# Attention stage on whole 1152-column PSUM regions, with unsplit float32 projections

## The chip, the cores and the metric

The kernel runs on one core of one Trainium2 chip. The metric is the device time of one execution in microseconds (us). The core has a matrix engine (TensorE, "PE" in the profile; "PEld" are its weight loads), a vector engine (VectorE, "DVE"), a scalar engine (ScalarE, "ACT"), GpSimd ("POOL") and a queue engine that issues DMAs (SyncE, "SP"). SBUF is the on-chip memory of 128 partitions; PSUM is the small memory that TensorE writes into, of 8 banks, each 512 float32 wide. TensorE's clock has two levels, 1.2 and 2.4 GHz; the profile gives the granted clock of a stretch as a share of the higher one.

## The reference

Batch 8, 8 heads, 576 tokens, head dimension 64. The stage that changes is the first, a linear attention:

```python
def phi(x):                                   # x: (b, h, 576, 64), w_phi: (64, 128)
    proj = einsum('bhsd,df->bhsf', x, w_phi)
    proj = proj - max(abs(proj), axis=-1, keepdims=True)
    return concatenate([exp(proj), exp(-proj)], axis=-1)
q_p, k_p = phi(q), phi(k)
kv  = einsum('bhsf,bhsd->bhfd', k_p, v)
z   = sum(k_p, axis=2)
num = einsum('bhsf,bhfd->bhsd', q_p, kv)
den = einsum('bhsf,bhf->bhs', q_p, z)[..., None] + 1e-6
out = num / den
```

Two feed-forward stages follow (a gated one with a 576 x 576 spatial product, then a low-rank token mixing and a channel network of width 2048). All is float32.

## The kernel before, in words

The heads are worked two at a time: 32 pairs, one turn of the loop in `attention` (L516) for each. A framework turns the program into five in-order instruction streams: it plans an order by program order, readiness and its own costs, allocates tiles from named rings (a tag with `bufs` buffers) and places the waits. `issue_after(x)` keeps what stands under it behind instruction x.

A pair's 576 tokens are 4 full tiles of 128 tokens and a tail of 64; the tails of both heads share one 128-token tile, so a pair has 9 blocks of 128 tokens x 128 features, 1152 columns in all. In one turn for pair p the program issues, in this order: the loads of q and k of pair p+1; `queries(p)`; `key_values(p-1)`; `keys(p)`; `outputs(p-1)`; `transposed_queries(p)`; `finish(p-2)` on GpSimd; `reciprocals(p-1)`; and one weight job (a piece of a later stage's weights: DMA, unpacking at L55 to L72, split), of which there are 29.

- `split_pair` (L364) makes a high and a low float32r part of each 128 x 640 input, one copy on VectorE and one subtraction on GpSimd.
- `project` (L373) multiplies with a block-diagonal weight for both heads at once (256 columns), three matmuls for each full tile (high-high, low-high, high-low) and three of 128 columns for the tail: 15 matmuls for q (tile names pq) and 15 for k (pk). They go to PSUM in three parts of 512, 512 and 128 columns; each part has one absolute maximum (L392) and one subtraction (L397) on VectorE.
- `keys` (L404): two exponentials for each part on ScalarE into kp. `key_values` (L445): 18 float32 matmuls into pkv, then a split into kv.
- `transposed_queries` (L415): 9 transposes by TensorE (pt), then for each of three parts and both signs an exponential in float32r (L440), the same in float32 (L441) and their difference on VectorE (L442), into qp.
- `outputs` (L468): 24 float32r matmuls (pn) in four groups of six, each copied out by ScalarE (L482). The denominators take a round through DRAM (L484, L494, L496); `finish` multiplies (L507) and stores x by one DMA (L513).

PSUM is one pool for the whole kernel, with two rings of four one-bank buffers: "a" (pq, pk, pt and the float32 exponentials e) and "b" (pkv, pn).

Of the kernel before, what the change touches and what calls it, by code (L numbers as in the profile page):

```python
# [9 lines left out]
F32 = mybir.dt.float32  # L10
F32R = mybir.dt.float32r
# [7 lines left out]
P = 128  # L19
# [59 lines left out]
class Mixer:  # L79
# [3 lines left out]
    def __init__(self, tc, ctx, aps):  # L83
        self.tc, self.nc, self.ctx = tc, tc.nc, ctx
        self.__dict__.update(aps)
        self.B, self.NP = self.qT.shape[:2]
        self.D, self.F = self.w_phi.shape[0] // 2, self.w_phi.shape[1] // 3
        self.S = self.U.shape[0]
# [244 lines left out]
    def alloc_attention(self, es):  # L333
        tc, nc = self.tc, self.nc
        D, F = self.D, self.F
        self.af = es.enter_context(tc.tile_pool(name="af", bufs=1))
        ap = self.ap = es.enter_context(tc.tile_pool(name="ap", bufs=1))

        self.wph, self.wst = (
            [ap.tile([P, n], F32R, name=f"{m}{i}") for i in range(2)]  # L340
            for m, n in (("wph", 2 * F), ("wst", F))
        )
        wz = self.stage("wz", 3 * F)
        nc.scalar.dma_start(wz, self.w_phi)
        self.split(self.wph[0], self.wph[1], wz[:, : 2 * F], ehi="dve", elo="dve")
        self.split(self.wst[0], self.wst[1], wz[:, 2 * F :])
        self.st = {}
# [15 lines left out]

    def split_pair(self, p, w):  # L364
        x = [
            self.ap.tile([P, self.NST * P], F32R, tag=f"{w}s{i}", name=f"{w}s{i}_{p}", bufs=1)
            for i in range(2)
        ]
        lo = self.split(x[0], x[1], self.st[p][w], ehi="dve", elo="pool" if p else "dve")
        self.last[3] = lo.ins  # L370
        self.st[p][w] = x

    def project(self, p, w):  # L373


        nc, F, NF = self.nc, self.F, self.NF
        hi, lo = self.st[p][w]
        res = []
        for t0 in range(0, self.NST, 2):
            tiles = range(t0, min(t0 + 2, self.NST))  # L380
            n = sum(2 if t < NF else 1 for t in tiles)
            pa = self.psum(f"p{w}{p}_{t0}").rearrange("p (u f) -> p u f", f=F)
            for t in tiles:
                cols = slice(t * P, (t + 1) * P)
                at = 2 * (t - t0)
                out, ws = (
                    (pa[:, at : at + 2, :], self.wph) if t < NF else (pa[:, at, :], self.wst)
                )
                for i, (x, y) in enumerate(((hi, 0), (lo, 0), (hi, 1))):
                    nc.tensor.matmul(out, x[:, cols], ws[y], start=(i == 0), stop=(i == 2))  # L390
            m = self.ap.tile([P, 4, 1], F32, tag="m", name=f"m{w}{p}_{t0}", bufs=6)
            nc.vector.tensor_reduce(  # L392
                out=m[:, :n, :], in_=pa[:, :n, :], op=ALU.max, axis=AX.X,
                apply_absolute_value=True,
            )
            s = self.ap.tile([P, 4, F], F32, tag=f"s{w}", name=f"s{w}{p}_{t0}", bufs=3)
            nc.vector.tensor_tensor(  # L397
                out=s[:, :n, :], in0=pa[:, :n, :],
                in1=m[:, :n, :].to_broadcast([P, n, F]), op=ALU.subtract,
            )  # L400
            res.append((2 * t0, n, s))
        return res

    def keys(self, p):  # L404
        nc, F = self.nc, self.F
        kp = self.ap.tile([P, 2 * self.NF + 1, 2, F], F32, tag="kp", name=f"kp{p}", bufs=1)
        for u0, n, s in self.project(p, "k"):
            for i, sign in enumerate((1.0, -1.0)):
                nc.scalar.activation(kp[:, u0 : u0 + n, i, :], s[:, :n, :], AF.Exp, scale=sign)  # L409
        self.st[p]["kp"] = kp  # L410
# [4 lines left out]
    def transposed_queries(self, p):  # L415
        nc, F, NF, S, tail = self.nc, self.F, self.NF, self.S, self.tail
        pts = [self.psum(f"pt{p}_{j}") for j in range(3)]
        for u0, n, s in reversed(self.st[p]["sq"]):
            for u in range(n):
                t, j = divmod(u0 + u, 2)  # L420
                out = pts[j][:, t * P : (t + 1) * P] if t < NF else pts[2][:, :P]
                nc.tensor.transpose(out, s[:, u, :], self.ident)
        qp = [
            self.ap.tile([P, 2, 2, S], F32R, tag=f"qp{i}", name=f"qp{i}_{p}", bufs=1)
            for i in range(2)
        ]


        for j in (2, 0, 1):
            if j < 2:  # L430
                src = pts[j]
                hi, lo = ([q[:, j, i, : NF * P] for i in range(2)] for q in qp)
                es = [self.psum(f"e{p}_{j}"), src]
            else:
                r3 = lambda a: a.rearrange("p (h s) -> p h s", h=2)
                src = r3(pts[2][:, :P])
                hi, lo = ([q[:, :, i, NF * P :] for i in range(2)] for q in qp)
                es = [r3(pts[2][:, P : 2 * P]), src]
            for i, sign in enumerate((1.0, -1.0)):
                nc.scalar.activation(hi[i], src, AF.Exp, scale=sign)  # L440
                self.last[0] = nc.scalar.activation(es[i], src, AF.Exp, scale=sign).ins  # L441
                nc.vector.tensor_tensor(out=lo[i], in0=es[i], in1=hi[i], op=ALU.subtract)  # L442
        self.st[p]["qp"] = qp

    def key_values(self, p):  # L445
        nc, D, NF = self.nc, self.D, self.NF
        kp, vb = self.st[p]["kp"], self.st[p]["v"]
        D1 = D + 1
        pkv = self.psum(f"pkv{p}", "b")[:, : 4 * D1].rearrange("p (i j d) -> p i j d", i=2, j=2)
        for i in range(2):  # L450
            nc.tensor.matmul(
                pkv[:, i], kp[:, 2 * NF, i, :], vb[:, 2 * NF * D1 :], start=True, stop=False
            )
            for j in range(2):
                for t in range(NF):
                    u = 2 * t + j
                    nc.tensor.matmul(  # L457
                        pkv[:, i, j, :], kp[:, u, i, :], vb[:, u * D1 : (u + 1) * D1],
                        start=False, stop=(j == 1 and t == NF - 1),
                    )  # L460
        kv = [
            self.ap.tile([P, 2, 2, D1], F32R, tag=f"kv{i}", name=f"kv{i}_{p}", bufs=2)
            for i in range(2)
        ]
        self.split(kv[0], kv[1], pkv, elo="dve")
        self.st[p]["kv"] = kv

    def outputs(self, p):  # L468
# [4 lines left out]
        for j in range(2):  # L473
            for c in range(2):
                pn = self.psum(f"pn{p}_{j}_{c}", "b")
                for n, (k, q, i) in enumerate(terms):
                    nc.tensor.matmul(  # L477
                        pn[: D + 1, :HS], kv[k][:, i, j, :],
                        qp[q][:, j, i, c * HS : (c + 1) * HS],
                        start=(n == 0), stop=(n == len(terms) - 1),  # L480
                    )
                nc.scalar.copy(nd[:, j, c, :], pn[: D + 1, :HS])  # L482
# [18 lines left out]
    def finish(self, p, eng):  # L501
# [4 lines left out]
        for j in range(2):  # L506
# [5 lines left out]
            )  # L512
        nc.sync.dma_start(self.xd[b][:, hp, :], x)  # L513
        del self.st[p]

    def attention(self, jobs):  # L516
        n = self.B * self.NP
        late, rest, work = self.NP + 3, [], None
        self.load_pair(0)
        self.split_pair(0, "q")  # L520
        self.split_pair(0, "k")
        for p in range(n + 1):
            if p + 1 < n:
                self.load_pair(p + 1)
            if p < n:
                self.queries(p)
                if p + 1 < n:
                    self.split_pair(p + 1, "q")
            if p:
                self.key_values(p - 1)  # L530
            if p < n:
                self.load_values(p)
                self.keys(p)
                if p + 1 < n:
                    self.split_pair(p + 1, "k")
            if p:
# [482 lines left out]
```

## Time and profile before

| | us |
|---|---|
| median of 3 runs (1825.13 to 1828.86) | 1827.36 |
| the profiled execution | 1825.05 |
| its span, first to last instruction | 1822.9 |
| mean granted clock over the span | 0.976 |

The span is what the trace covers; the 2.15 us beside it lie around it. Times inside the trace count from the span's start. A matmul's duration holds its way through the array and overlaps that of the next, so a stream's cost is read from start to start. A float32 matmul leaves two records and two weight loads, a float32r matmul or a transpose one.

### The profile page before, as it was taken

To read this page: it belongs to the slowest core of one execution; us is meant where nothing else is said; L and a number is where in the kernel's file an instruction comes from. 1 tells how busy PE (TensorE), PEld (TensorE's weight loads), DVE (VectorE), ACT (ScalarE), POOL (GpSimd) and SP (SyncE) were. 2 spreads that over 40 slices of the span, in tenths; PEclk is the share of its full clock that TensorE was granted. 3 is DMA by queue.
4 is the path that set the end of the run, shared out by engine and by line. 5 is a ranking of instruction groups with operands and counts; after the bars stand their busy time and mean duration, and the time that the engine had idled before them with its cause. 6 is when DMAs were issued, how large, how long until landed. Compare 5 with 4: busy or idle time off the path is not lost.

```text
span 1822.9 us, 27191 instructions
## 1 busy us (share of the span) xinstructions
PE 1731.4 (95%) x10632; PEld 1644.4 (90%) x10632; DVE 894.0 (49%) x1750; ACT 648.3 (36%) x1509; POOL 433.4 (24%) x367
## 2 busy tenths in 40 slices
PE   7888888888899999999999999999999999999999
PEld 7787888787898888888889899999999999999999
DVE  6889988788866566665653721211211210211211
ACT  4666665666654443443343411111201201211210
POOL 1445444444434342333332010000000000000000
PEclk8999899999999999999999999999999999999999
DMA  3444444434212332332221620110110110110100
GB/s 121 127 117 129 128 117 135 119 111 122 81 43 76 117 117 94 111 112 90 78 89 56 187 64 1 35 36 1 35 35 1 35 35 1 35 35 4 32 18 18
DMA packets 78468, 132.14 MB, mean 72 GB/s; under 512 B 17090, under 2 KB 39778, under 8 KB 78340
## 3 DMA queue, kind: packets, MB, share of 16 engines
q1 hardware_dynamic: 78196, 130.21, 23.4%
q8 instruction: 84, 1.38, 0.3%
q14 instruction: 44, 0.36, 0.1%
q10 hardware_dynamic: 144, 0.20, 0.0%
HBM read 93.38 MB, written 36.85 MB: 71 GB/s over the span
## 4 chain that ended last, share of the span: by engine, by line
PE 60%; DMA 7%; DVE 6%; ACT 3%; POOL 2%; issue 1%; SPq 0%; DVEq 0%; POOLq 0%; ACTq 0%
PE pc L582 22%; PE ph L582 21%; DMA raw_c<-in_w_ch 5%; PE pv L582 4%; PE px L582 3%; PE pu L582 3%; PE pt L785 1%; PE pz L582 1%; PE py L789 1%; PE pkv L457 1%; DMA den<-nd 1%; PE pn L477 1%; ACT kp L409 1%; POOL xs L617 1%; DVE qp L442 1%
## 5 line engine op out<-in xcount | busy, mean ns | idle before, releaser
L582 PE MATMUL pc<-h,w 128*128 128x384 f32 x2304 | 403.8, 335 | 0.0
L582 PEld LDWEIGHTS pc<-h,w 128*128 128x128 f32 x2304 | 402.0, 188 | 0.0
L582 PE MATMUL ph<-us,w 128*128 128x384 f32 x2244 | 391.0, 334 | 0.0
L582 PEld LDWEIGHTS ph<-us,w 128*128 128x128 f32 x2244 | 389.2, 188 | 0.0
L833 ACT ACTIVATE h<-ph 128x384 fp32r<-128x384 f32 x187 | 91.9, 492 | 631.3 <-PE ph L582 631.3
L834 DVE SCALAR_TENSOR_TENSOR h<-ph,h 128x384 fp32r<-128x384 f32 x187 | 104.2, 557 | 275.2 <-ACT h L833 275.1
L121 POOL TENSOR_TENSOR us<-u,us 128x384 fp32r<-128x384 f32 x48 | 49.3, 1061 | 682.3 <-ACT us L118 673.3
L869 DVE TENSOR_TENSOR u<-pc,u 128x384 f32<-128x384 f32 x48 | 25.5, 557 | 364.1 <-PE pc L582 364.1
L457 PE MATMUL pkv<-v,kp 128*128 128x65 f32 x1024 | 139.6, 296 | 0.0
L457 PEld LDWEIGHTS pkv<-v,kp 128*128 128x128 f32 x1024 | 138.0, 216 | 0.0
L477 PE MATMUL pn<-qp,kv 128*65 128x288 f32 x768 | 119.3, 298 | 7.4 <-DVE kv L121 4.9
L582 PE MATMUL pz<-wt,vn 128*128 128x288 f32 x768 | 112.6, 295 | 1.2 <-DVE u L727 1.2
L477 PEld LDWEIGHTS pn<-qp,kv 128*65 128x65 f32 x768 | 97.9, 137 | 14.4 <-DVE kv L121 10.1
L582 PEld LDWEIGHTS pz<-wt,vn 128*128 128x128 f32 x768 | 105.2, 188 | 2.1 <-DVE u L727 1.9
L440 ACT ACTIVATE qp<-pt 128x128 fp32r<-128x128 f32 (+1 forms) x192 | 93.7, 493 | 35.5 <-DVE qp L442 32.8
L582 PE MATMUL px<-wo,g 128*128 128x512 f32 x384 | 94.1, 403 | 11.7 <-ACT g L118 11.7
L582 PEld LDWEIGHTS pu<-xs,wi 128*128 128x128 f32 x768 | 102.7, 188 | 0.7
L582 PE MATMUL pu<-xs,wi 128*128 128x288 f32 x768 | 103.2, 295 | 0.0
L582 PEld LDWEIGHTS px<-wo,g 128*128 128x128 f32 x384 | 72.9, 194 | 30.4 <-ACT g L118 14.3
L507 POOL TENSOR_TENSOR x<-nd,rec 64x576 f32<-64x576 f32 x62 | 91.9, 1482 | 15.2 <-ACT nd L482 10.2
L582 PE MATMUL pv<-wi,xs 128*128 128x512 f32 x384 | 92.3, 393 | 0.0
L390 PE MATMUL pq<-wph,qs 128*128 128x256 f32 x384 | 72.2, 341 | 17.5 <-DVE qp L442 9.3
(152 smaller groups left out, 2333.2 us busy)
## 6 DMA issues: line engine op xcount, KB each, us to landing
raw_c<-in_w_ch SPq DMA_DIRECT2D x32, 512.0 KB, 4.4
v<-in_v SPq DMA_DIRECT2D x32, 325.0 KB, 3.0
q<-in_qT SPq DMA_DIRECT2D x32, 320.0 KB, 2.9
k<-in_kT SPq DMA_DIRECT2D x32, 320.0 KB, 3.0
rec<-rd SPq DMA_DIRECT2D x32, 288.0 KB, 3.7
xd<-x SPq DMA_DIRECT2D x32, 288.0 KB, 2.1
x<-xd SPq DMA_DIRECT2D x32, 288.0 KB, 3.0
outT<-u SPq DMA_DIRECT2D x48, 192.0 KB, 1.9
```

What stands on the lines that cost most here:

```text
L121: return (nc.gpsimd if elo == "pool" else nc.vector).tensor_tensor(out=lo, in0=src, in1=hi, op=ALU.subtract)
L390: nc.tensor.matmul(out, x[:, cols], ws[y], start=(i == 0), stop=(i == 2))
L409: nc.scalar.activation(kp[:, u0 : u0 + n, i, :], s[:, :n, :], AF.Exp, scale=sign)
L440: nc.scalar.activation(hi[i], src, AF.Exp, scale=sign)
L442: nc.vector.tensor_tensor(out=lo[i], in0=es[i], in1=hi[i], op=ALU.subtract)
L457: nc.tensor.matmul(pkv[:, i, j, :], kp[:, u, i, :], vb[:, u * D1 : (u + 1) * D1], start=False, stop=(j == 1 and t == NF - 1),)
L477: nc.tensor.matmul(pn[: D + 1, :HS], kv[k][:, i, j, :], qp[q][:, j, i, c * HS : (c + 1) * HS], start=(n == 0), stop=(n == len(terms) - 1),)
L507: eng.tensor_tensor(out=x[j * D : (j + 1) * D, :], in0=nd[:D, j].rearrange("p c s -> p (c s)"), in1=rec[:, j * S : (j + 1) * S], op=ALU.mult,)
L582: self.nc.tensor.matmul(out, x, y, start=(start and i == 0), stop=(stop and i == len(terms) - 1))
L833: nc.scalar.activation(h[:, 0, :], ph, AF.Relu)
L834: nc.vector.scalar_tensor_tensor(out=h[:, 1, :], in0=ph, scalar=0.0, in1=h[:, 0, :], op0=ALU.max, op1=ALU.subtract,)
L869: nc.vector.tensor_tensor(out=u[:, f, :], in0=pcs[f], in1=u[:, f, :], op=ALU.add)
```

## The change

The weight is no longer block-diagonal but the 64 x 128 weight stacked twice; q and k are used as they are loaded. Each head is multiplied within its own 64 rows (partitions 0 to 63 or 64 to 127) by one float32 matmul of 128 columns; the tail tile uses all 128 rows. The whole projection lies in one PSUM region of three banks, with one maximum, one subtraction and one exponential per sign over 1152 columns. The transposes fill another three-bank region, in an order that puts the tail between the heads. Of the two differences of the queries' exponentials one goes to GpSimd. The attention's PSUM has a pool of its own: one region "pa" (q, then k), one "pt", and a ring of two banks "b"; the later stages' pool is made after the attention. The store of x becomes three DMAs. The weight jobs stand behind the last exponential and VectorE's difference of the turn.

```diff
-        self.ps = ctx.enter_context(tc.tile_pool(name="ps", bufs=1, space=PSUM))   # __init__
+        self.pp = es.enter_context(tc.tile_pool(name="pp", bufs=1, space=PSUM))    # alloc_attention
+        self.wst = ap.tile([P, F], F32, name="wst")
+        nc.scalar.dma_start(self.wst, self.w_phi)
-    def split_pair(self, p, w):
...
+    def wide(self, name, tag):
+        t = self.pp.tile([P, 12, P], F32, tag=tag, name=name, bufs=1)
+        return t[:, : 2 * self.NF + 1, :]
     def project(self, p, w):
-                for i, (x, y) in enumerate(((hi, 0), (lo, 0), (hi, 1))):
-                    nc.tensor.matmul(out, x[:, cols], ws[y], start=(i == 0), stop=(i == 2))
+        n = 2 * NF + 1
+        pa = self.wide(f"p{w}{p}", "pa")
+        x, ws = self.st[p][w], self.wst
+        for t in range(NF):
+            cols = slice(t * P, (t + 1) * P)
+            for j in range(2):
+                d = slice(j * D, (j + 1) * D)
+                nc.tensor.matmul(
+                    pa[:, j * NF + t, :], x[d, cols], ws[d, :], start=True, stop=True
+                )
+        nc.tensor.matmul(pa[:, 2 * NF, :], x[:, NF * P :], ws, start=True, stop=True)
+        m = self.ap.tile([P, n, 1], F32, tag="m", name=f"m{w}{p}", bufs=2)
+        nc.vector.tensor_reduce(
+            out=m, in_=pa, op=ALU.max, axis=AX.X, apply_absolute_value=True
+        )
+        s = self.ap.tile([P, n, F], F32, tag=f"s{w}", name=f"s{w}{p}", bufs=1)
+        nc.vector.tensor_tensor(
+            out=s, in0=pa, in1=m.to_broadcast([P, n, F]), op=ALU.subtract
+        )
+        return s
     def keys(self, p):
+        s = self.project(p, "k")
+        kp = self.ap.tile([P, 2, 2 * self.NF + 1, F], F32, tag="kp", name=f"kp{p}", bufs=1)
+        for i, sign in enumerate((1.0, -1.0)):
+            nc.scalar.activation(kp[:, i], s, AF.Exp, scale=sign)
     def transposed_queries(self, p):
+        pt = self.wide(f"pt{p}", "pt")
+        for u in (*range(NF), 2 * NF, *range(NF, 2 * NF)):
+            at = u if u < NF else NF if u == 2 * NF else u + 1
+            nc.tensor.transpose(pt[:, at, :], s[:, u, :], self.ident)
+        pt = pt.rearrange("p u f -> p (u f)")
...
+        e = self.ap.tile([P, 2 * S], F32, tag="e", name=f"e{p}", bufs=1)
+        nc.scalar.activation(qp[0][:, 0, :], pt, AF.Exp)
+        nc.scalar.activation(e, pt, AF.Exp)
+        lo = nc.gpsimd.tensor_tensor(out=qp[1][:, 0, :], in0=e, in1=qp[0][:, 0, :], op=ALU.subtract)
+        nc.scalar.activation(qp[0][:, 1, :], pt, AF.Exp, scale=-1.0)
+        self.last[0] = nc.scalar.activation(pt, pt, AF.Exp, scale=-1.0).ins
+        d = nc.vector.tensor_tensor(out=qp[1][:, 1, :], in0=pt, in1=qp[0][:, 1, :], op=ALU.subtract)
+        self.last[1], self.last[2] = d.ins, lo.ins
     def key_values(self, p), outputs(self, p):
-        pkv = self.psum(f"pkv{p}", "b") ... pn = self.psum(f"pn{p}_{j}_{c}", "b")
+        pkv = self.pp.tile([P, 512], F32, tag="b", name=f"pkv{p}", bufs=2)
+                pn = self.pp.tile([P, 512], F32, tag="b", name=f"pn{p}_{j}_{c}", bufs=2)
     def finish(self, p, eng):
-        nc.sync.dma_start(self.xd[b][:, hp, :], x)
+        nc.sync.dma_start(self.xd[b][:D, hp, :], x[:D, :])
+        nc.sync.dma_start(self.xd[b][D:, hp, :full], x[D:, S - full :])
+        nc.sync.dma_start(self.xd[b][D:, hp, full:], x[D:, : S - full])
     def attention(self, jobs):
-            with self.tc.issue_after(self.last[3]):
+            with self.tc.issue_after(self.last[0]), self.tc.issue_after(self.last[1]):
                 if work:
                     work = work()
-                with self.tc.issue_after(self.last[0]):
-                    rest = [f() for f in rest]
+                rest = [f() for f in rest]
     def alloc_moe(self, left, right):
+        self.ps = self.ctx.enter_context(
+            tc.tile_pool(name="ps", bufs=1, space=PSUM, reuse_waits="tile")
+        )
-        return np.block([[w, z, w], [z, w, w]])
+        return np.concatenate([w, w], axis=0)
```

## Rows read from the trace of the kernel before

**Rows 1.** Windows: stretch, length; busy us (records) by engine, clock, DMA share, GB/s.

```profile
24.00:504.00 480.00, 417.68 (x3011) 390.06 (x3011) 409.14 (x799) 301.91 (x769) 209.57 (x151) 0.93 0.40 117
...
1200.00:1400.00 200.00, 200.00 (x1152) 200.00 (x1151) 32.99 (x60) 28.54 (x60) 11.80 (x12) 1.00 0.07 24
```

**Rows 2.** Line 451: ns min/median/max of one, first and last start us.

```profile
L451 PE MATMUL pkv<-v,kp x128: 275/329/587, 16.4 to 510.5; 128*128 128x130 f32 x128
```

**Rows 3.** Timeline of TensorE, one turn at the upper clock: start, us.

```profile
300.11 1.59 PE L390 MATMUL pk<-wph,ks 128*128 128x256 f32 x12
301.54 0.30 PE L477 MATMUL pn<-qp,kv 128*65 128x288 f32 x1
301.67 0.45 PE L390 MATMUL pk<-wst,ks 128*128 128x128 f32 x3
301.96 0.30 PE L422 MATMUL pt<-ident,sq 128*128 128x128 f32 x1
302.14 2.59 PE L477 MATMUL pn<-qp,kv 128*65 128x288 f32 x18
304.57 1.03 PE L422 MATMUL pt<-ident,sq 128*128 128x128 f32 x8
306.71 0.49 PE L451 MATMUL pkv<-v,kp 128*128 128x130 f32 x2 [1.11 <-ACT kp L409]
307.04 1.90 PE L457 MATMUL pkv<-v,kp 128*128 128x65 f32 x16
308.77 0.44 PE L451 MATMUL pkv<-v,kp 128*128 128x130 f32 x2
309.05 1.90 PE L457 MATMUL pkv<-v,kp 128*128 128x65 f32 x16
310.75 0.95 PE L390 MATMUL pq<-wph,qs 128*128 128x256 f32 x6
```

**Rows 4.** Waits of TensorE, 24 to 504 us: total us, times, longest.

```profile
PE pkv L451 <- ACT kp L409: 33.4, 30, 1.2
```

**Rows 5.** Windows of 4 us: a stretch whose clock falls.

```profile
488.00:492.00 4.00, 2.89 (x24) 2.65 (x22) 3.96 (x8) 3.53 (x9) 3.84 (x4) 1.00 0.01 2
...
496.00:500.00 4.00, 4.00 (x20) 4.00 (x20) 2.33 (x6) 3.04 (x7) 0.00 (x0) 0.50 0.06 9
```

**Rows 6.** Tile pt, 600 to 900 us: weight loads of 64 rows; idle before them.

```profile
L785 PEld LDWEIGHTS pt<-ident,x x90: 134/139/144, 642.7 to 897.2; 128*128 128x128 f32 x72, 64*128 64x128 f32 x18
...
  issue: 3.0, 18
```

**Rows 7.** Groups of instructions by form, 24 to 504 us, VectorE: busy us, mean ns.

```profile
L392 DVE TENSOR_REDUCE mq<-pq 128x4 f32<-128x512 f32 x62 | 42.3, 682 | 15.1 <-PE pq L390 14.9
L442 DVE TENSOR_TENSOR qp<-e,qp 128x512 fp32r<-128x512 f32 x60 | 41.2, 687 | 7.4 <-ACT e L441 7.4
L59 DVE SCALAR_TENSOR_TENSOR bits_wi<-raw_wi,bits_wi 128x256 int32<-128x256 int32 x15 | 24.4, 1628 | 0.5
L120 DVE CAST ks<-k 128x640 fp32r<-128x640 f32 x30 | 19.6, 654 | 0.0
L55 DVE TENSOR_SCALAR bits_wi<-raw_wi 128x256 int32<-128x256 int32 x15 | 19.6, 1308 | 0.0
L442 DVE TENSOR_TENSOR qp<-pt,qp 128x128 fp32r<-128x128 f32 x60 | 17.3, 288 | 24.0 <-ACT pt L441 23.9
```

**Rows 8.** The same view, ScalarE.

```profile
L440 ACT ACTIVATE qp<-pt 128x512 fp32r<-128x512 f32 x120 | 72.3, 603 | 0.0
L440 ACT ACTIVATE qp<-pt 128x128 fp32r<-128x128 f32 x60 | 16.4, 274 | 32.8 <-DVE qp L442 32.8
```

**Rows 9.** The same view, GpSimd.

```profile
L121 POOL TENSOR_TENSOR ks<-k,ks 128x640 fp32r<-128x640 f32 x30 | 47.6, 1587 | 4.0 <-PE pn L477 1.8
L121 POOL TENSOR_TENSOR wi<-w_wi,wi 128x256 fp32r<-128x256 f32 x16 | 11.8, 736 | 111.5 <-ACT wi L118 111.5
```

**Rows 10.** The line that stores x, 24 to 504 us: issue ns min/median/max.

```profile
L513 SPq DMA_DIRECT2D xd<-x x29: 326/327/327, 50.6 to 491.8; - x29
```

More of the change, by code (lines that the diff above doesn't have):

```diff
@@ L86, in __init__ @@
         self.B, self.NP = self.qT.shape[:2]
-        self.D, self.F = self.w_phi.shape[0] // 2, self.w_phi.shape[1] // 3
+        self.D, self.F = self.w_phi.shape[0] // 2, self.w_phi.shape[1]
         self.S = self.U.shape[0]
@@ L335, in alloc_attention @@
         D, F = self.D, self.F
+        self.pp = es.enter_context(tc.tile_pool(name="pp", bufs=1, space=PSUM))
         self.af = es.enter_context(tc.tile_pool(name="af", bufs=1))
         ap = self.ap = es.enter_context(tc.tile_pool(name="ap", bufs=1))
[L339 to L346, printed above, removed]
+        self.wst = ap.tile([P, F], F32, name="wst")
+        nc.scalar.dma_start(self.wst, self.w_phi)
         self.st = {}
@@ L362, in load_values @@
         self.st[p]["v"] = vb
-    def split_pair(self, p, w):
[L365 to L371, printed above, removed]
-    def project(self, p, w):
[L376 to L387, printed above, removed]
-                )
-                for i, (x, y) in enumerate(((hi, 0), (lo, 0), (hi, 1))):
-                    nc.tensor.matmul(out, x[:, cols], ws[y], start=(i == 0), stop=(i == 2))
[L391 to L402, printed above, removed]
@@ L415, in transposed_queries @@
     def transposed_queries(self, p):
[L416 to L422, printed above, removed]
+        nc, F, NF, S = self.nc, self.F, self.NF, self.S
@@ L423, in transposed_queries @@
+        s = self.st[p]["sq"]
+        pt = self.wide(f"pt{p}", "pt")
[3 more added lines that the diff above has]
+        pt = pt.rearrange("p u f -> p (u f)")
         qp = [
-            self.ap.tile([P, 2, 2, S], F32R, tag=f"qp{i}", name=f"qp{i}_{p}", bufs=1)
+            self.ap.tile([P, 2, 2 * S], F32R, tag=f"qp{i}", name=f"qp{i}_{p}", bufs=1)
@@ L425, in transposed_queries @@
             for i in range(2)
         ]
[L429 to L442, printed above, removed]
+        e = self.ap.tile([P, 2 * S], F32, tag="e", name=f"e{p}", bufs=1)
@@ L448, in key_values @@
         D1 = D + 1
-        pkv = self.psum(f"pkv{p}", "b")[:, : 4 * D1].rearrange("p (i j d) -> p i j d", i=2, j=2)
+        pkv = self.pp.tile([P, 512], F32, tag="b", name=f"pkv{p}", bufs=2)
+        pkv = pkv[:, : 4 * D1].rearrange("p (i j d) -> p i j d", i=2, j=2)
         for i in range(2):
             nc.tensor.matmul(
-                pkv[:, i], kp[:, 2 * NF, i, :], vb[:, 2 * NF * D1 :], start=True, stop=False
+                pkv[:, i], kp[:, i, 2 * NF, :], vb[:, 2 * NF * D1 :], start=True, stop=False
             )
@@ L457, in key_values @@
                     nc.tensor.matmul(
-                        pkv[:, i, j, :], kp[:, u, i, :], vb[:, u * D1 : (u + 1) * D1],
+                        pkv[:, i, j, :], kp[:, i, j * NF + t, :], vb[:, u * D1 : (u + 1) * D1],
                         start=False, stop=(j == 1 and t == NF - 1),
@@ L512, in finish @@
             )
-        nc.sync.dma_start(self.xd[b][:, hp, :], x)
+        full = self.NF * P
+        nc.sync.dma_start(self.xd[b][:D, hp, :], x[:D, :])
+        nc.sync.dma_start(self.xd[b][D:, hp, :full], x[D:, S - full :])
+        nc.sync.dma_start(self.xd[b][D:, hp, full:], x[D:, : S - full])
         del self.st[p]
@@ L983, in rows, with stacked @@
         )
-    def diagonal(w):
-        z = np.zeros_like(w)
-        return np.block([[w, z, w], [z, w, w]])
+    def stacked(w):
+        return np.concatenate([w, w], axis=0)
     arrays = {
@@ L993 @@
         "v": rows(inputs["v"]),
-        "w_phi": diagonal(inputs["w_phi"]),
+        "w_phi": stacked(inputs["w_phi"]),
         "w_in": inputs["moe_w_in"],
```

14 lines of the change are left out of this document (2 added, 12 removed).

## The prediction

> **What bounds the kernel now.** I read the windows first. From 24 to 504 us, the attention, TensorE is 418 of 480 us busy, VectorE 409, ScalarE 302; at 1200 us TensorE is busy throughout at full clock and the others hardly [rows 1]. So the change can act on the attention alone, and behind it TensorE sets the time: what a turn of the loop gains shows in the total, once for each of 31 intervals.
>
> How long is a turn? Line 451 runs four times for each of 32 pairs, from 16.4 to 510.5 us [rows 2]; its two halves lie 2.06 us apart (306.71 and 308.77), and the two records of one matmul 0.14 [rows 3]. (510.5 - 0.14 - 2.06 - 16.4) / 31 = 15.87 us.
>
> What does TensorE need of it? The timeline of one turn at the upper clock, from start to start [rows 3]: pkv 306.71 to 310.75, 4.04 us. A projection: twelve matmuls of 256 columns in 1.43 (0.12 each), three of 128 in 0.29, together 1.72; there are two, 3.44. Eighteen pn in 2.43, so 24 take 3.24. Eight transposes end 1.03 after their start, the last one's own 0.27 to 0.30 within that: 0.11 each, nine in 0.98. Sum 11.7 us. So 4.2 of 15.87 us are not matmul work. 33.4 us in 30 turns, 1.1 each, are waits of pkv for the key exponentials [rows 4]: a chain from VectorE's subtraction through ScalarE. Another 1.1 is the clock, 0.93 on the mean, 7% of the turn [rows 1]. A fall looks like this: TensorE is 2.89 of 4 us busy from 488 us, at 1.00, and by 496 us it runs at 0.50, the 1.2 GHz level [rows 5]. The other 2.0 are shorter waits. VectorE, 409.14 / 30.2 = 13.5 us a turn, is almost as full as the turn is long, so what stands in its queue is late for TensorE.
>
> **The change part by part.**
>
> *Projection.* 15 float32r matmuls become 8 + 1 float32 ones, 18 records of 128 columns. Nearest rows: records of 130 columns, 0.14 each by the second pair (308.77 to 309.05) and 0.165 by the first (306.71 to 307.04), and records of 65 columns, 0.106 (16 in 1.70) [rows 3]. I take 0.12, nearer the two cheap ones because the 0.165 follows a wait: 18 x 0.12 = 2.16. If the two heads' matmuls, in different rows, ran side by side, a record would cost half of 0.106, the lower end. Going to 64 rows and back: weight loads of 64 rows stood 3.0 us idle in 18 cases, 0.17 each, with no releaser [rows 6]; two changes a projection, 0.34. A projection 2.5, plus 0.78 each, 1.56 a turn. Floor of a turn: 11.7 + 1.56 = 13.3 us.
>
> The Trainium skill, "TensorEngine Tiling (Array Packing)", section Tiling Modes, says that changing the tiling mode drains TensorE. That speaks against this change, and the trace agrees: 0.17 us each [rows 6].
>
> *VectorE.* 687 ns at 512 and 288 at 128 columns [rows 7]: 1.04 ns a column and 0.155 fixed, so 1.35 us at 1152. No row shows one instruction over three banks; bounds are this, and one more fixed part at each of two borders, 1.66. I take 1.35. Maxima and subtractions: 8 x 0.68 + 4 x 0.28 = 6.6 becomes 4 x 1.35 = 5.4. Differences of the queries: 4 x 0.687 + 2 x 0.288 = 3.3 becomes one, 1.35. Two copies, 0.65 at most each, go [rows 7]. Together about 4.3 less: 9.2 us a turn.
>
> *ScalarE.* 603 at 512, 274 at 128 [rows 8]: 1.15 us at 1152 (1.48 with a fixed part for each border). Key exponentials, 4 x 0.60 + 2 x 0.27 = 2.9, become 2.3; queries', 5.9, become 4.6. Of 10.0 us a turn about 8 remain; no bound.
>
> *GpSimd.* 1587 at 640 and 736 at 256 columns [rows 9]: the new difference takes 2.7 us, two of 1.59 go. It is on the way to the outputs, beside two more exponentials (2.3) and VectorE's 1.35, so it hides; uncovered it would add 2.7.
>
> *One region for both projections.* The next projection must wait until the subtraction has read the last. Worked from t = 0, the end of the key subtraction of pair p-1: the query projection (2.5) now stands where TensorE waited for the key exponentials, which end at 2.3; pkv 2.5 to 6.55; maximum and subtraction of q 2.6 to 5.3, under pkv; key projection to 9.05; outputs to 12.3; transposes to 13.3. Query exponentials of p-1 2.3 to 6.9, GpSimd's difference by 7.3, VectorE's by 8.35, both before the outputs. Keys' maximum and subtraction 9.2 to 11.9, 1.4 us ahead of the next projection. So the wait of 1.1 is gone, and late next is VectorE. The weight jobs are held until its difference, 8.35, and two of their instructions alone take 1.31 + 1.63 [rows 7]: they end at 11.3, the key subtraction at 14.0. Plus 0.7 in a turn with such a job.
>
> *Ring of two instead of four.* A group of outputs is 6 x 0.135 = 0.81; its copy must end before the next but one, with 0.81 to spare. ScalarE is idle there in the order above, so nothing; with a query exponential of 1.15 ahead, 0.3 to 0.7.
>
> *Clock.* Idle ahead of pkv is what the fall showed, and that goes; I keep 0.5 of 1.1.
>
> *Stores.* Two more issues a turn, 2 x 0.327 = 0.65 of SP's time [rows 10], hidden as long as no load stands late behind them; 21 us in 32 turns if all did. The moved jobs' loads stand behind them in the same queue. Later stages: nothing, TensorE is full there.
>
> Sum: 13.3 + 0.7 + 0.5 = 14.5 us a turn; (15.87 - 14.5) x 31 = 42.5 us less. From the profiled execution, 1825.05: 1782.5. That execution lies 2.3 below the median of the runs shown; I put the forecast at 1783, a little over the sum.
>
> **The rivals.**
>
> *A, side by side.* The 64-row matmuls overlap: 16 x 0.053 + 2 x 0.12 + 0.34 = 1.4 a projection, floor 11.1. Then VectorE bounds turns with jobs: key maximum and subtraction behind the jobs end at 14.0 as before, and 12.0 without. About 13.3 with the clock: 80 us less, 1745. For it: different rows, different banks. Against: weight loads may still come one by one, and pkv's records of 65 columns cost hardly less than those of twice the width [rows 3]. The Trainium skill says in the page and section named that tiles run weight loads and matmuls in parallel; no run here shows it yet. Chance 0.17.
>
> *B, slower: pkv stays ahead of the query projection.* The planner keeps today's order, pkv before pq [rows 3]. With one region TensorE then has little to do while it is read: exponentials 2.3, pkv 4.04, projection 2.5, outputs 3.24 while q is subtracted, projection 2.5, then 2.7 of keys' maximum and subtraction with only transposes beside: 17.3 us, 1.4 x 31 = 44 more, 1870. It is slower as soon as more than 15.87 - 13.3 = 2.6 of the 5.0 us of exponentials and key subtraction lie bare. For it: today's order, and single buffers. Against: the query projection comes first in the program and its region is free 2.3 us before the exponentials end. Chance 0.18.
>
> *C, dear records.* 0.14 to 0.165 us: floor 14.0 to 14.9, with 0.7 and 0.5 a turn of 15.2 to 16.1; 1804 to 1832, and no gain at 1825. For it: the rows of nearly that width. Chance 0.15.
>
> **How the numbers follow.** Forecast 0.50 (1760 to 1805), A 0.17, C 0.15, B 0.18. Faster by over 0.2% (what measurement can tell from no change): forecast, A and 0.05 of C, 0.72. Within 0.2%: 0.06 of C. Slower: B and 0.04 of C, 0.22. The range, 1730 to 1838, takes in A, C and the start of B; some 0.18 lies outside, nearly all above.
>
> **What would show it.** Pairs of pkv 14 to 15 us apart; pq starting before pkv; float32 projection records 0.12 us apart (half of that: A; 0.14 or more: C); VectorE near 9 us a turn; a higher clock before 504 us; the stage behind as long as now. The prediction is wrong if TensorE idles before projections for the subtraction, if instructions over three banks cost more than one fixed part, or if the clock falls in the float32 stretches without idle time before.

## The result and the profile after

The changed kernel took 1749.01 us (median of 4 runs, 1746.84 to 1751.04), the kernel before 1826.24 beside it: ratio 0.9576, 95% interval 0.9555 to 0.9597, 77 us less. That is inside the range, 34 below the forecast of 1783, and 4 from the 1745 of rival A. The profiled execution took 1747.03 us, its span is 1745.2, its granted clock 0.988.

The windows row of the attention in the kernel after (stretch, length; busy us and records of PE, PEld, DVE, ACT, POOL; clock; DMA share; GB/s), which answers to the first of [rows 1]:

```profile
24.00:430.00 406.00, 361.34 (x3209) 333.31 (x3207) 277.26 (x348) 276.94 (x420) 193.30 (x123) 0.97 0.51 138
```

And the line of the first pkv matmul of a group (ns min/median/max, first and last start), which answers to [rows 2]:

```profile
L432 PE MATMUL pkv<-v,kp x128: 275/276/378, 17.0 to 425.9; 128*128 128x130 f32 x128
```

Worked as for the kernel before, a turn is (425.9 - 0.14 - 2.06 - 17.0) / 31 = 13.12 us where it was 15.87: 85 us gained in the loop. From the last pkv record to the end the kernel before takes 1822.9 - 510.5 = 1312.4 us, the kernel after 1745.2 - 425.9 = 1319.3: 7 given back. The clock in the attention is 0.97, was 0.93.

The timeline of TensorE in the kernel after, one turn at the upper clock (start, us; in brackets the idle time before, and what ended it); it answers to [rows 3]:

```profile
292.21 1.16 PE L374 MATMUL pq<-wst,q 64*128 64x128 f32 x16
293.31 0.49 PE L377 MATMUL pq<-wst,q 128*128 128x128 f32 x2
293.63 0.39 PE L432 MATMUL pkv<-v,kp 128*128 128x130 f32 x2
293.86 1.90 PE L438 MATMUL pkv<-v,kp 128*128 128x65 f32 x16
295.59 0.44 PE L432 MATMUL pkv<-v,kp 128*128 128x130 f32 x2
295.87 1.90 PE L438 MATMUL pkv<-v,kp 128*128 128x65 f32 x16
297.69 1.16 PE L374 MATMUL pk<-wst,k 64*128 64x128 f32 x16
298.78 0.49 PE L377 MATMUL pk<-wst,k 128*128 128x128 f32 x2
299.09 0.48 PE L458 MATMUL pn<-qp,kv 128*65 128x288 f32 x2
300.46 1.20 PE L407 MATMUL pt<-ident,sq 128*128 128x128 f32 x9 [0.89 <-DVE qp L421]
301.45 3.10 PE L458 MATMUL pn<-qp,kv 128*65 128x288 f32 x22
305.00 1.16 PE L374 MATMUL pq<-wst,q 64*128 64x128 f32 x16 [0.45 <-PE pn L458]
```

From start to start: sixteen 64-row records in 1.10 us (292.21 to 293.31), 0.069 each; a whole projection 1.42 and 1.40; pkv 4.06; the outputs 0.48 + 3.10; nine transposes 0.99. Sum 11.45 us of work in a turn of 12.79; 0.89 + 0.45 are waits. The query projection stands ahead of pkv.

The mean of 0.069 mixes two prices. The same timeline in narrow windows shows single starts; each line is one window, and the window is chosen so that it holds only the records that still run in it:

```profile
292.21 0.38 PE L374 MATMUL pq<-wst,q 64*128 64x128 f32 x2
292.43 0.39 PE L374 MATMUL pq<-wst,q 64*128 64x128 f32 x4
293.10 0.28 PE L374 MATMUL pq<-wst,q 64*128 64x128 f32 x2
293.31 0.38 PE L377 MATMUL pq<-wst,q 128*128 128x128 f32 x1
293.52 0.28 PE L377 MATMUL pq<-wst,q 128*128 128x128 f32 x1
```

The records come in pairs, 0.01 us apart: a record lasts 0.27, two of them together 0.28. The first experiment below shows that a pair is one record of each head. From the second pair (292.43) to the eighth (293.10) a pair takes 0.112 us, so a record 0.056. Where the rows change, the steps are longer: 0.21 from the first pair to the second, 0.21 from the last pair to L377, 0.21 to L377's second record, and 0.20 from the last transpose (292.01) to the first pair, where transposes follow each other in 0.11. Beyond the usual step that is 0.10 + 0.10 + 0.10 + 0.09 = 0.39 us for the two changes of a projection.

The waits of TensorE in the kernel after, 20 to 430 us (total us, times, longest), which answer to [rows 4]:

```profile
PE pn L458 <- POOL qp L418: 17.4, 19, 1.8
PE pt L407 <- DVE qp L421: 9.6, 10, 2.4
PE pk L374 <- issue: 5.4, 2, 4.0
PE pk L374 <- PE pkv L438: 4.1, 7, 1.0
PE pn L458 <- ACT kv L117: 3.4, 10, 1.5
PE pkv L432 <- ACT kp L393: 1.6, 2, 1.1
```

The 33.4 us of pkv's wait for the key exponentials are down to 1.6. The two largest are waits for the differences of the query exponentials, GpSimd's (L418) and VectorE's (L421); before, it was the query projection that stood for VectorE's (L442), 12.3 us in 23 times between 24 and 504 us. The six rows sum to 41.5 us, 1.3 a turn.

Groups by form in the kernel after, 24 to 430 us (busy us, mean ns | idle before), which answer to [rows 7 to 9]:

```profile
L379 DVE TENSOR_REDUCE mk<-pk 128x9 f32<-128x1152 f32 x31 | 41.9, 1351 | 0.9 <-PE pk L377 0.9
L472 DVE TENSOR_SCALAR den<-den 128x9 f32<-128x9 f32 x31 | 21.2, 683 | 31.9 <-DMA den<-nd 31.9
L55 DVE TENSOR_SCALAR bits_wi<-raw_wi 128x256 int32<-128x256 int32 x16 | 11.2, 698 | 0.0
L59 DVE SCALAR_TENSOR_TENSOR bits_wi<-raw_wi,bits_wi 128x256 int32<-128x256 int32 x16 | 10.1, 634 | 0.0
L416 ACT ACTIVATE qp<-pt 128x1152 fp32r<-128x1152 f32 x31 | 34.6, 1115 | 0.0
L418 POOL TENSOR_TENSOR qp<-e,qp 128x1152 fp32r<-128x1152 f32 x31 | 81.4, 2626 | 16.7 <-ACT e L417 13.0 <-issue 2.9 <-POOL x L488 0.6
```

Instructions over 1152 columns cost 1.35 us on VectorE and 1.12 on ScalarE, where they read three banks: one fixed part, none per bank. GpSimd's difference, which reads SBUF alone, costs 2.63. VectorE is busy 277.26 / (406 / 13.12) = 9.0 us a turn.

Two turns of the kernel after across the engines (the same columns) show how the new waits come about:

```profile
282.14 0.45 SPq L497 DMA_DIRECT2D xd<-x  x1
...
282.68 0.55 SPq L465 DMA_DIRECT2D den<-nd  x1
...
284.89 0.17 DVE L472 TENSOR_SCALAR den<-den 128x9 f32<-128x9 f32 x1 [2.97 <-DMA den<-nd]
...
285.23 1.31 DVE L421 TENSOR_TENSOR qp<-pt,qp 128x1152 fp32r<-128x1152 f32 x1
...
286.59 1.60 PE L407 MATMUL pt<-ident,sq 128*128 128x128 f32 x7 [1.38 <-DVE qp L421]
...
296.27 2.62 POOL L418 TENSOR_TENSOR qp<-e,qp 128x1152 fp32r<-128x1152 f32 x1 [1.18 <-issue]
...
297.99 0.94 DVE L472 TENSOR_SCALAR den<-den 128x9 f32<-128x9 f32 x1 [1.41 <-DMA den<-nd]
```

VectorE's difference L421 stands in its queue behind L472, the small addition to the denominators, and that waits for a DMA (L465) which SP issues behind a store of x (L497). In the first turn VectorE stands 2.97 us and the transposes 1.38. In the second L472 itself takes 0.94 instead of 0.17 us and ends at 298.93, 0.04 after GpSimd's L418 at 298.89. Both are turns in which SP issues that DMA late; in most turns it does not, as shown below.

### The profile page after: what moved, and what is told of

It is laid out like the page before. It is cut to its first block, busy times and chain, and to the rows that moved or that the text cites. A ratio compares the mean times of both kernels' runs of the same rounds, so it can differ in the third digit from the quotient of the medians.

```text
span 1745.2 us, 26552 instructions
## 1 busy us (share of the span) xinstructions
PE 1672.0 (96%) x10824; PEld 1584.4 (91%) x10824; DVE 752.8 (43%) x1266; ACT 613.4 (35%) x1124; POOL 413.7 (24%) x336
## 4 chain that ended last, share of the span: by engine, by line
PE 63%; DMA 6%; DVE 2%; ACT 2%; POOL 1%; issue 0%; SPq 0%; DVEq 0%; POOLq 0%; ACTq 0%
PE pc L563 23%; PE ph L563 22%; PE pv L563 4%; PE px L563 4%; DMA raw_c<-in_w_ch 4%; PE pu L563 3%; PE pt L766 1%; POOL xs L598 1%; DMA x<-xd 1%; PE py L770 1%; PE pz L563 1%; PE pv L574 1%; PE px L574 1%; PE pr L744 1%; ACT low_c L67 0%
## 5 line engine op out<-in xcount | busy, mean ns | idle before, releaser
L120 POOL TENSOR_TENSOR us<-u,us 128x384 fp32r<-128x384 f32 x48 | 49.2, 1051 | 682.3 <-ACT us L117 673.5
L458 PE MATMUL pn<-qp,kv 128*65 128x288 f32 x768 | 127.3, 312 | 24.1 <-POOL qp L418 18.0
L458 PEld LDWEIGHTS pn<-qp,kv 128*65 128x65 f32 x768 | 104.8, 143 | 34.4 <-POOL qp L418 23.1
L488 POOL TENSOR_TENSOR x<-nd,rec 64x576 f32<-64x576 f32 x62 | 87.1, 1405 | 195.4 <-DMA rec<-rd 99.1
L438 PE MATMUL pkv<-v,kp 128*128 128x65 f32 x1024 | 121.3, 272 | 0.0
L438 PEld LDWEIGHTS pkv<-v,kp 128*128 128x128 f32 x1024 | 119.4, 192 | 0.0
L463 ACT COPY nd<-pn 65x288 f32<-65x288 f32 x128 | 50.0, 394 | 133.7 <-issue 73.0
L418 POOL TENSOR_TENSOR qp<-e,qp 128x1152 fp32r<-128x1152 f32 x32 | 84.0, 2626 | 34.3 <-ACT e L417 30.5
```

The source lines that it names most:

```text
L120: return (nc.gpsimd if elo == "pool" else nc.vector).tensor_tensor(out=lo, in0=src, in1=hi, op=ALU.subtract)
L418: lo = nc.gpsimd.tensor_tensor(out=qp[1][:, 0, :], in0=e, in1=qp[0][:, 0, :], op=ALU.subtract)
L438: nc.tensor.matmul(pkv[:, i, j, :], kp[:, i, j * NF + t, :], vb[:, u * D1 : (u + 1) * D1], start=False, stop=(j == 1 and t == NF - 1),)
L458: nc.tensor.matmul(pn[: D + 1, :HS], kv[k][:, i, j, :], qp[q][:, i, (2 * j + c) * HS : (2 * j + c + 1) * HS], start=(n == 0), stop=(n == l ...
L488: eng.tensor_tensor(out=x[j * D : (j + 1) * D, :], in0=nd[:D, j].rearrange("p c s -> p (c s)"), in1=rec[:, j * S : (j + 1) * S], op=ALU.mult,)
```

## The experiments

Turns are worked from the pkv line as above; "waits" are TensorE's between 20 and 430 us. All times stand against the kernel before, run beside them, so two edits compare by their ratios; the change has 0.9576 (0.9555 to 0.9597).

### One head after the other

```diff
-        for t in range(NF):
-            for j in range(2):
+        for j in range(2):
+            for t in range(NF):
```

> The changed kernel, but each projection issues all four tiles of one head and then all four of the other, so that neighbouring matmuls use the same 64 rows. Side by side (rival A of the prediction): the 16 records of 64 rows take 0.068 us each now because two heads overlap; in turn they cost what full-row records cost, 0.106 to 0.11, 0.6 to 0.7 us more a projection, 1.3 a turn; where TensorE sets the turn this is 40 us more, about 1789. Rival: a record of 64 rows is cheap by itself; then the pitch stays at 0.068 and the time at 1749.

1758.31 us (ratio 0.9636, 0.9598 to 0.9675); turn 13.38. The timeline of TensorE in this kernel:

```profile
304.30 1.71 PE L374 MATMUL pq<-wst,q 64*128 64x128 f32 x16
305.94 0.49 PE L377 MATMUL pq<-wst,q 128*128 128x128 f32 x2
```

Sixteen records take 1.64 us, 0.1025 each, and two neighbours no longer start together. In a narrow window:

```profile
304.51 0.38 PE L374 MATMUL pq<-wst,q 64*128 64x128 f32 x2
```

Two records of 0.27 us last 0.38 together, so the second starts 0.11 after the first: one record of the same rows costs what a pair of different rows costs in the change (three of the sixteen, where the two heads meet, still start beside another). So records of different rows do run side by side. The order also changes the banks: in the change neighbours write to two banks, here to one. Different banks alone are not enough, since L377's second record and pkv's first, both of all rows and in different banks, start 0.11 apart (293.52 and 293.63); different rows in one bank were not tried. In turn, the records cost 1.0 us a turn more of TensorE's work, but the turn grows by 0.26 alone: the waits for L421 and L418 fall from 27.0 to 9.8 us. TensorE's work is not the only bound of the turn.

### The projection alone

The kernel before with unsplit queries and keys and the 64-row matmuls, still in one-bank parts:

```diff
-                for i, (x, y) in enumerate(((hi, 0), (lo, 0), (hi, 1))):
-                    nc.tensor.matmul(out, x[:, cols], ws[y], start=(i == 0), stop=(i == 2))
+                nc.tensor.matmul(
+                    pas[j][:, t, :], x[d, cols], ws[d, :], start=True, stop=True
+                )
```

> The kernel before with only the new projection: q and k unsplit in float32, each head in half the rows, head 0 in one bank, head 1 in a second, the tail in a third; rings of four one-bank buffers, parts of 512, 512 and 128 columns, differences on VectorE as before. TensorE needs 0.8 us less a turn, VectorE loses two copies (about 1.1), GpSimd two subtractions. If VectorE's queue sets the old turn: about 1 us a turn, 1793. If the projection is most of the gain: below 1775. If the gain comes from the regions and their order: above 1810.

1815.81 us (0.9944, 0.9919 to 0.997), turn 15.66; pkv still waits 24.5 us for the key exponentials. Less work on TensorE, and the two copies and two subtractions of the split gone from VectorE and GpSimd, give about 10 us (0.3 to 0.8%).

### The regions alone

The kernel after with the old split and the 15 float32r matmuls of a projection:

```diff
-                nc.tensor.matmul(
-                    pa[:, j * NF + t, :], x[d, cols], ws[d, :], start=True, stop=True
-                )
+            for i, (x, y) in enumerate(((hi, 0), (lo, 0), (hi, 1))):
+                nc.tensor.matmul(out, x[:, cols], ws[y], start=(i == 0), stop=(i == 2))
```

> The changed kernel with the old projection: split float32r inputs, 15 matmuls a projection, everything else as in the change (three-bank regions, single instructions over 1152 columns, difference on GpSimd, job placement, three stores). Floor of TensorE 11.7 us, with the changed kernel's waits of 1.4 about 13.1 to 13.9 a turn: 1760 to 1775. Rival: GpSimd now has the two splits (1.6 each) beside the difference (2.6) and the products (2.9), and what waits for it grows: 15 us a turn, 1805 or more.

1781.26 us (0.9766, 0.9723 to 0.9809), turn 13.88, pkv's wait for the exponentials 1.6 us. The regions alone give 43 us, the projection alone 10, both together 77. The likely reason that the two give more than their sum: with the splits, VectorE is busy 336.88 of 406 us and the key projection waits 17.0 us for the query subtraction; without them it is busy 277.26 us and that wait ("issue" before pk) is 5.4. That was not tested further.

### Rival B's order

```diff
+                    with self.tc.issue_after(self.last[3]):   # the last pkv matmul
+                        self.queries(p)
```

> The changed kernel, with the query projection held behind pkv of the pair before, the order that the kernel before has. Rival B's sum with the measured projection of 1.3: 2.3 + 4.04 + 1.3 + 3.24 + 1.3 + 2.7 = 14.9 us a turn, 1.8 more than the 13.1 measured, 1805. If the waits on the exponentials are hidden by something else, no more than 0.5 a turn, below 1765.

1979.72 us (1.0848, 1.0808 to 1.0889), clock 0.69 in the attention, turn 20.6. The timeline of TensorE, and then the windows row of these 8 us:

```profile
303.22 0.80 PE L432 MATMUL pkv<-v,kp 128*128 128x130 f32 x2 [3.35 <-ACT kp L393]
303.81 3.52 PE L438 MATMUL pkv<-v,kp 128*128 128x65 f32 x16
```

```profile
303.00:311.00 8.00, 7.78 (x36) 7.77 (x36) 2.50 (x2) 3.60 (x5) 4.62 (x3) 0.50 0.14 37
```

The order that rival B feared is slow, and more than its 17.3 us a turn: after 3.35 us of idle time the clock is 0.50, the 1.2 GHz level, and sixteen records of pkv take 3.32 us (303.81 to 307.13) where they took 1.73. The rival left that out. With the query projection behind pkv nothing of the gain is left.

### Every wide instruction cut in three

Maxima, subtractions, exponentials and VectorE's difference in pieces of 512, 512 and 128 columns; then ScalarE's alone, and VectorE's alone.

```diff
-        nc.scalar.activation(e, pt, AF.Exp)
+        for c in (slice(0, 512), slice(512, 1024), slice(1024, 1152)):
+            nc.scalar.activation(e[:, c], pt[:, c], AF.Exp)
```

> The changed kernel with its regions, order and engines, but each maximum, subtraction and exponential (and VectorE's difference) cut into 512, 512 and 128 columns. If the single instructions carry the gain: VectorE about 1.0 and ScalarE about 1.5 us more a turn, both on the chain from projection to exponentials; 1 us or more a turn, 1780 or more. If the gain is that the projections no longer share buffers with the exponentials, so that the query projection runs ahead of pkv: below 1762.

> Only ScalarE's exponentials are cut into 512, 512 and 128 columns; VectorE keeps its instructions over 1152. Six exponentials a turn, two cuts each, of about 0.17 us: ScalarE has 2.0 us a turn more, about 10 of 13.1. If ScalarE is off the path, as the forecast has it, the time is that of the change, 1745 to 1752. If the exponentials are on the path (two of four ahead of each difference), 0.7 to 1.4 us a turn, 1770 to 1792, and the outputs wait longer for GpSimd's difference. With all engines cut it was 1812.

> Only VectorE's maxima, subtractions and difference are cut into 512, 512 and 128 columns; ScalarE keeps its instructions over 1152. Ten more instructions a turn of 0.155 us fixed: VectorE has 1.55 us a turn more, 10.6 of 13.1. If that alone is the price of the cut: at most 1.55 x 31 = 48 more, 1749 to 1797; at the upper end VectorE bounds the turn. If the pieces change the order in which the planner sets VectorE's queue (a later copy ahead of the last subtraction), the price is that of the all-cut version, 1800 to 1815, with VectorE's own wait for ScalarE in the trace. If neither, 1745 to 1755, and the cut of ScalarE carried it.

All: 1812.19 us (0.9919, 0.9888 to 0.9951), turn 15.32. ScalarE alone: 1806.5 (0.9926, 0.9903 to 0.9949), turn 15.14. VectorE alone: 1792.34 (0.9841, 0.9816 to 0.9866), turn 14.59. Neither growth can be read as the price of the pieces. ScalarE has 267.74 / (406 / 15.14) - 276.94 / (406 / 13.12) = 1.0 us more work a turn, VectorE 284.88 / (406 / 14.59) - 9.0 = 1.2 us; the turns grow by 2.0 and 1.5. The waits of VectorE in the kernel with ScalarE cut:

```profile
DVE kv L120 <- ACT kv L117: 44.2, 16, 6.1
```

VectorE's subtraction for kv now stands ahead of its difference in every turn, and in about every other turn the key maximum does too (L120 at 291.93, L379 at 293.56, the difference L427 at 294.84): VectorE waits 44.2 us in 16 turns for kv's copy, and the outputs 26.6 us in 26 turns for the difference. The kernel after has both behind the difference (L421 at 285.23, L120 at 286.82, L379 at 287.16). With VectorE cut, the timeline of one turn:

```profile
211.40 2.32 DVE L477 TENSOR_SCALAR den<-den 128x9 f32<-128x9 f32 x1 [5.22 <-DMA den<-nd]
...
213.89 0.63 DVE L381 TENSOR_REDUCE mq<-pq 128x4 f32<-128x512 f32 x1
...
216.80 0.29 DVE L384 TENSOR_TENSOR sq<-pq,mq 128x128 f32<-128x128 f32 x1
...
217.19 1.90 PE L374 MATMUL pk<-wst,k 64*128 64x128 f32 x16 [3.98 <-issue]
```

The denominators' addition now stands ahead of the maximum of the queries, where the kernel after has it behind; here it waits 5.22 us for its DMA and lasts 2.32, and the key projection waits 3.98 us until the subtraction has read the shared region (it ends at 217.09); the records then take 1.90 us instead of 1.16, at a mean clock of 0.61 from 217 to 219 us. Such waits ("issue" before pk) are 32.4 us in 11 turns, 5.4 in 2 in the kernel after. The pieces changed the planner's order, and the new waits are those of the new order; what the pieces cost with the order kept was not measured.

### The reciprocals held back

```diff
-                self.reciprocals(p - 1)
+                with self.tc.issue_after(self.last[1]):   # VectorE's difference
+                    self.reciprocals(p - 1)
```

> The changed kernel with the two reciprocal instructions held behind VectorE's difference of the queries. In the changed kernel VectorE stood 31.9 us for the denominators' DMA, with the difference behind it, and TensorE 9.6 us for that difference. If these waits set the turn: 0.2 to 0.4 us a turn, 1736 to 1743. If the wait only moves to GpSimd's difference (17.4 us of waits): 1749.

1757.57 us (0.966, 0.962 to 0.9699), turn 13.63: slower than the change, against the expectation. The wait of the transposes for L421 goes from 9.6 to 0.5 us, as meant, but pkv waits 20.4 us for the key exponentials again: another order, another chain.

### One store instead of three

Head 1's product is written in token order by two instructions, so one DMA stores both heads:

```diff
-        nc.sync.dma_start(self.xd[b][:D, hp, :], x[:D, :])
-        nc.sync.dma_start(self.xd[b][D:, hp, :full], x[D:, S - full :])
-        nc.sync.dma_start(self.xd[b][D:, hp, full:], x[D:, : S - full])
+        nc.sync.dma_start(self.xd[b][:, hp, :], x)
```

> The changed kernel with one store of x instead of three: the products of the second head are written in token order by two instructions instead of one. The prediction put the two extra stores at nothing. If they make the denominators' DMA late (it stands behind two of them in SP's queue): 0.2 to 0.5 us a turn, 1733 to 1743. If nothing: 1749, or up to 5 more for the extra GpSimd instruction.

1737.65 us (0.953, 0.9506 to 0.9554), turn 12.71: faster than the change by 11 us of the medians, 8 by the ratios, and the fastest kernel of the study. GpSimd has one instruction more, and its product is cut another way, so the edit tests more than the count of the stores.

### Both differences on VectorE

```diff
-        lo = nc.gpsimd.tensor_tensor(out=qp[1][:, 0, :], in0=e, in1=qp[0][:, 0, :], op=ALU.subtract)
+        lo = nc.vector.tensor_tensor(out=qp[1][:, 0, :], in0=e, in1=qp[0][:, 0, :], op=ALU.subtract)
```

> The changed kernel with both differences of the query exponentials on VectorE. GpSimd's took 2.6 us and the outputs waited for it 17.4 us (0.56 a turn); on VectorE it takes 1.35 and adds them to a queue of 9 us a turn. If that wait sets the turn: 1732 to 1745. If VectorE's queue then makes the projections late: 1755 to 1775.

1743.27 us (0.9557, 0.9531 to 0.9582), not clear of noise from the change. The wait for GpSimd is gone, but the transposes now wait 21.8 us for L421, and the turn is 13.20, no shorter; the profiled execution gains its time behind the last pkv record (1743.5 - 429.5 = 1314.0 us, 1319.3 in the change). On the path of the loop GpSimd's 2.6 us cost nothing that VectorE would not cost as well.

### One store, and both on VectorE

The two edits above together.

> The product of head 1 is written in token order and stored with head 0 by one DMA, and the difference of the low parts stands on VectorE instead of GpSimd. Alone, the first gave 1737.6 and the second 1743.3, against 1749.0 for the change. If they shorten different waits (the denominators' DMA on SP's queue; the outputs' wait for GpSimd) the gains add: 1749 - 11.4 - 5.7 = 1732, and the turn is 12.5 us. If both only shorten the one chain that ends with VectorE's difference, the larger one remains: 1736 to 1740. If VectorE, with 1.35 us more in its queue in each turn and another product, has become the bound: 1745 or more, and the wait of the transposes for its difference is longer than 21.5 us in the attention.

1753.22 us (0.963, 0.9607 to 0.9653), turn 13.37. They don't add; together they are slower than the change. The transposes wait less than in the last kernel (14.9 us, 21.8 there), so it is not VectorE's difference that became later; "issue" before pk, the wait for the query subtraction, has grown to 13.5 us in 7 turns (9.4 in 6 there), and the clock is 0.95.

### The first weight job let free

```diff
+            if work:
+                work = work()
             with self.tc.issue_after(self.last[0]), self.tc.issue_after(self.last[1]):
-                if work:
-                    work = work()
```

> The first weight job of a turn is no longer held until the query exponentials and VectorE's difference are issued; the second still is. The forecast put 0.7 us a turn on jobs that stand behind the difference and ahead of the key subtraction. If that holds, a job that can stand earlier gives up to 0.7 x 16 turns = 11 us back, 1738 to 1749. If jobs now stand ahead of the difference, outputs and transposes wait for it instead: 1.3 us in 16 turns or more, 1755 to 1780, and the wait of the transposes for VectorE's difference grows from 9.6 us. If the int32 instructions of the jobs cost more beside GpSimd's difference than alone (698 and 634 ns in the change, 1308 and 1628 before), their mean rises above 1000 ns when they are let run beside it.

1764.78 us (0.9698, 0.9678 to 0.9717), turn 13.53. Slower. The waits of VectorE:

```profile
DVE bits_wi L55 <- DMA raw_wi<-in_w_in: 40.0, 14, 4.2
DVE bits_wo L55 <- DMA raw_wo<-in_w_out: 18.4, 7, 3.6
```

The jobs stand at the head of VectorE's queue before their loads have landed, 58 us in 21 turns, ahead of the query maximum; "issue" before pk is 27.1 us in 12 turns. In the change, held back, VectorE's part of the jobs waits 0.9 us for a load. Their own length grew too, by less: 16 instructions of L59 take 1240 instead of 634 ns, 9.7 us in all.

## Why the prediction came out as it did

**Where it was right.** The turn, not the stage behind, carried the gain. The query projection went ahead of pkv, and pkv's wait went (33.4 to 1.6 us); with the order undone the kernel is slower than before. VectorE 9.0 us a turn (9.2 forecast), wide instructions 1.35, 1.12 and 2.63 us (1.35, 1.15, 2.7), the clock 0.97 (half of the loss kept).

**The term that was mis-sized.** "I take 0.12" for a record of the projection. Measured: 0.056, two records side by side in 0.112, which is the forecast's own sign of rival A ("half of that: A"); the rival had 0.053. The other term, "two changes a projection, 0.34", was near: 0.39, of which 0.09 lie ahead of the first record. From start to start a projection takes 1.42 us where 2.5 was forecast, and the floor is 11.45 us, not 13.3. So rival A, with a chance of 0.17, was right about the projection in both its terms. The Trainium skill, "TensorEngine Tiling (Array Packing)", section Tiling Modes, says that tiles load weights and multiply in parallel, and that a change of mode drains the engine; the trace agrees on the first (0.112 us for two records of different rows, 0.11 for one where neighbours share their rows) and on the second (0.39 us for two changes).

**The sum of a turn.** The reading of the old turn was already loose: "the other 2.0 are shorter waits", but the waits of TensorE beside pkv's sum to 28.5 us between 24 and 504 us, 0.95 a turn, so that 1 us of it stayed unexplained. In the kernel after: floor 11.45, waits 1.3, the rest (the clock most likely) 0.37: 13.12. Forecast 13.3 + 0.7 + 0.5. The turn's 1.38 us less than forecast are 43 us in 31 turns; the 7 us given back leave 36, which is what lies between the sum, 1782.5, and the profiled execution. The 0.7 was for weight jobs ahead of the key subtraction; jobs turned out cheaper (698 and 634 ns for the two instructions that were taken at 1308 and 1628), and the waits came from elsewhere: L421 behind the denominators' addition and its DMA, the outputs behind GpSimd's difference. And work and waits don't add as the forecast had it: with 1.0 us more of work (one head after the other) the turn grew by 0.26, since the waits shrank. That kernel pays 0.11 for most of its records, nearly the forecast's 0.12, and takes 9 us more than the change (11 by the ratios): the dear record explains about a third of the 34 us, more only if the rest of the forecast projection (2.5, against 1.96 there) would have cost more. The rest must come from the 0.7 and from adding up work and waits that lie beside each other; how much each was not separated. Rival A's time, 1745, is 4 us off partly by luck: its turn of 13.3 us came from the same weight jobs, and it gave nothing back behind the loop.

**Stores, "hidden as long as no load stands late behind them".** Not borne out: the kernel with one store is 8 to 11 us faster. Why is open. In the second turn shown above the denominators' DMA stands late: its input is whole at 294.10 (the last copy, 293.72 + 0.38), and SP issues it at 295.68, behind the store at 295.12, which waited for GpSimd's product. But this is not the rule, and one store does not change it. SP's waits for the copy before it issues that DMA, 20 to 430 us, in the change and then with one store:

```profile
SPq L465 <- ACT nd L463: 16.4, 18, 5.3
SPq L465 <- ACT nd L463: 23.2, 24, 5.3
```

In 18 turns of the change SP stands ready and issues it as the copy ends. Over 31 turns the issues lie 27.0 us behind the ends of the last copies, with one store 26.9, and the transposes wait 9.6 us for L421 in both. What fell is the outputs' wait for GpSimd's difference, from 17.4 to 10.2 us; GpSimd's products were cut another way too, so the part of the stores was not told apart.

**GpSimd, "so it hides".** Only in part: the outputs wait 17.4 us for it. But VectorE in its place gives no shorter turn.

**"Later stages: nothing".** 7 us were given back behind the last pkv record, at the handover. In the kernel before, matmuls of the next stage stand ahead of the last outputs; after, they follow them. The timelines of TensorE there, before:

```profile
512.27 2.32 PE L582 MATMUL pv<-wi,xs 128*128 128x512 f32 x9
514.43 3.33 PE L477 MATMUL pn<-qp,kv 128*65 128x288 f32 x24
```

and after:

```profile
432.76 5.01 PE L458 MATMUL pn<-qp,kv 128*65 128x288 f32 x22 [1.97 <-DVE kv L120]
437.61 11.16 PE L563 MATMUL pv<-wi,xs 128*128 128x512 f32 x48
```

The last turn's waits lie bare, and its outputs run at the lower clock, 0.50 from 432 to 437 us (22 records in 4.85 us; 24 took 3.17 at 1.00 before). That the second PSUM pool, made after the attention, keeps the next stage back is likely from the code and wasn't tried.

## What to carry to other kernels

Put neighbouring matmuls into different row halves before pricing them: the same sixteen records cost 1.10 or 1.64 us by their order alone, and each change between 64 and 128 rows about 0.2 us. Once waits have moved into an in-order queue, ask of each small instruction in it what it waits for: here a 0.17 us addition that waits for a DMA held the subtraction and the difference behind it, and the three edits after which a waiting instruction stood earlier in VectorE's queue (ScalarE cut, VectorE cut, the jobs let free) were all slower than the change. Two edits of which neither harms alone may harm together when a planner orders the queues: run the pair.

## What the runs showed of the hardware

A short VectorE instruction can last until a GpSimd instruction ends. Of the 31 additions L472 in the kernel after, nine took 0.17 us and the others 0.28 to 2.10, each of them beside a GpSimd instruction, and all 22 end 0.03 to 0.04 us after that instruction's end (so do all 21 with one store, and all 24 with both differences on VectorE). One of them, in the timeline:

```profile
56.28 2.61 POOL L418 TENSOR_TENSOR qp<-e,qp 128x1152 fp32r<-128x1152 f32 x1
...
57.79 1.13 DVE L472 TENSOR_SCALAR den<-den 128x9 f32<-128x9 f32 x1 [4.06 <-DMA den<-nd]
```

56.28 + 2.61 = 58.89, and 57.79 + 1.13 = 58.92. The mean of 683 ns is 0.5 us a turn above the 0.17 of L472 alone, just ahead of VectorE's difference. The weight jobs' L55 and L59 go the same way: 1308 and 1628 ns in [rows 7], 698 and 634 in the change, 385 and 410 with GpSimd's difference on VectorE, 771 and 1240 where they were let free. The Trainium skill, "SBUF — State Buffer", section Who interferes with whom, says that VectorE, in certain forms of instruction (tensor_scalar can be one, and those with two SBUF inputs are while GpSimd reads SBUF), shares a pair of ports with GpSimd, which the first to start holds for its whole instruction, while the other is blocked; these ends agree with it. What the stretch costs the whole kernel was not measured by a run of its own.

ScalarE's cut exponentials cost less than their fixed parts suggest: three pieces follow one another in 1.11 us (302.48 to 303.59 in the kernel with ScalarE cut), a whole one in 1.01 (295.02 to 296.03).
